# The words of the second MLP's weights loaded two steps in front instead of one, and four more of its weight tiles resident at its start

## The chip, the cores and the metric

The kernel runs on one core of one Trainium2 chip. The metric is the device time of one execution in microseconds (us), given as the median of several executions. The engines are named as the profile names them: PE (TensorE, the matmul engine), PEld (its weight loads), DVE (VectorE), ACT (ScalarE), POOL (GpSimd) and SP (SyncE); the last two issue most of the DMAs here.

## The reference, cut to what matters

Three parts follow one another: attention with a band mask (heads 0 to 3) and a dilated band mask (heads 4 to 7), an MLP that takes the maximum of three products, and an MLP with a rational activation.

```python
scores = (q @ k.T) / 8                      # 4 batches, 8 heads, 576 tokens, head size 64
scores = where(mask, scores, -1e9)          # 0 <= rel < 32; or 0 <= rel < 128 and rel % 4 == 0
attn = exp(scores - max); attn = attn / (attn.sum() + 1e-9)
x = (attn @ v)                              # arranged as 2304 tokens x 512

h = maximum(maximum(x @ w1, x @ w2), x @ w3)    # 512 -> 768
x = h @ w_out                                   # 768 -> 512

h = x @ w_in                                    # 512 -> 2048
P = a0 + a1*h + a2*h**2 + a3*h**3
Q = 1 + |b0|*|h| + |b1|*h**2
out = (P / (Q + 1e-6)) @ w_out2                 # 2048 -> 512
```

The weights come as 64-bit floating-point numbers. The kernel reads their raw words and makes 32-bit values of them itself.

## The kernel before, in words

Attention is cut into 12 chunks of 192 tokens (three a batch), the first MLP into units of 384, 384, 512, 512 and 512 tokens, the second MLP into 5 tiles of tokens by 16 slices of its inner size. Every value that enters an MLP's matmul is split into a high and a low part, and each product takes three matmuls (high by high, high by low, low by high: `mm3`, L581 to L586). An inner group of the first MLP is 12 matmuls, and its output group 18; a unit has 18 and 4 of them, which the code calls 22 slots. The order of each engine's instructions is the order in which the code emits them, moved by a scheduler that follows priorities; a block in `tc.high_priority(offset=-300)` has a lower one and is fitted in where its engine would be free.

Up to about 96 us a hand-written script mixes the first chunks of attention, unit 0, and the conversion of the first MLP's weights. Then units 1 to 4 follow. In units 1 to 3 the generator `attn(u + 1)` is advanced by one piece after each slot, so that the next unit's attention is computed between the groups: scores (L335), their masking, maximum and difference on DVE (L354 to L377), exponentials on ACT (L385), sums and scaling on DVE (L396 to L403), transposes on PE into the PSUM bank `tpp` (L414), their copy out of it on ACT to `pt` (L425), and the products with V (L437, L445), whose high part ACT writes to `x1h` (L462). For the MLP itself ACT copies one of three products to `m` (L604), DVE takes the maxima (L606), ACT and DVE split the result (`hhl`, L612 and L616), and ACT copies the unit's output to `xs` (L639).

Into the same units goes the conversion of the second MLP's 32 weight tiles of 128 by 512. A tile's steps are: `cv_load` issues a DMA of 512 KB on SP's queue that brings the raw words to a tile `raw`, of which there are two (L524); it is told to wait for the last matmul emitted so far (`PACE`); `cv_up` lets ACT turn the high words into `cvt` (L537); `cv_bits` does two operations on DVE (L543, L545), and `cv_lo` issues a DMA on POOL's queue that writes `cvt`, 256 KB, to scratch memory, `w2d` (L565). `cv_tick` (L573) advances all of these at once, each for another tile: 36 ticks over the 66 slots of units 1 to 3 (L770 to L773), in each of which tile k is loaded, tile k-1 goes through `cv_up`, k-2 through `cv_bits` and k-3 is written.

When unit 4 begins (L747 to L760), the space of conversion and attention is given back. The weight tiles come back from scratch by `load_w2` (L645): a DMA on SP's queue (L651), the high part by ACT (L652) and the low part by DVE (L653). Three are loaded there, and three more whenever one of the first MLP's six weight blocks is done with, 21 in all. The other 11 need the space of the pool `com`, which also holds `x1h` and `x1l`, the input of two units in turn; they are loaded when unit 4 has ended (L791 to L796), just ahead of the second MLP's first groups. Its work on a slice is one PE group into `h`, ACT and DVE operations (L819 to L856) that end in the high part `gh` (ACT, L851) and the low part `gl`, and the output matmuls (L870 to L872), which begin as soon as the first `gh` is there.

Of the kernel before, what the change touches and what calls it, by code (L numbers as in the profile page):

```python
# [7 lines left out]
F32 = mybir.dt.float32  # L8
F32R = mybir.dt.float32r
AF = mybir.ActivationFunctionType  # L10
# [93 lines left out]
def kernel(  # L104
# [16 lines left out]
    nc = tc.nc  # L121
# [35 lines left out]
    SBB = 1  # L157
    MB = 4
    LATE_CV = 300
    TICK = 36  # L160
    RAW2 = 2
    CVT2 = 2
    W2A = 3
# [5 lines left out]
    const = ctx.enter_context(tc.tile_pool(name="const", bufs=1))  # L169
    mm_p = ctx.enter_context(tc.tile_pool(name="mm", bufs=3, space=PSUM))  # L170

    com_es = ExitStack()
    com = com_es.enter_context(tc.tile_pool(name="com", bufs=1, reuse_waits="tile"))
    wo1_es = ExitStack()
# [45 lines left out]

    def unit_x1(u):
        if u not in x1:
            x1[u] = [com.tile([128, NP * T1], F32R, tag=tag, bufs=2, name=f"{tag}{u}")
                     [:, 0:NP * SZ1[u]].rearrange("p (c t) -> p c t", c=NP)
                     for tag in ("x1h", "x1l")]
        return x1[u]

    def load_k(b, part=None):

        if b not in at_k:  # L230
            if b == 0:
                for tag in ("x1h", "x1l"):
                    keys0[tag] = com.tile([128, NP * T1], F32, tag=tag, bufs=2, name="keys0")
                kTp, kTd = [keys0[tag][:, 0:2 * S] for tag in ("x1h", "x1l")]
            else:
                kTp, kTd = [at.tile([128, 2 * S], F32, tag=tag, name=f"{tag}{b}")
                            for tag in ("kTp", "kTd")]
            at_k[b] = (kTp.rearrange("p (n a t) -> p n a t", a=2, t=32),
                       kTd.rearrange("p (n m) -> p n m", n=8))
        kTp, kTd = at_k[b]  # L240
        queue = nc.sync if b < 2 else nc.gpsimd
        for k, cut in ((0, slice(0, CH // 32)), (2, slice(CH // 32, S // 32))):
            if part in (None, k):
                queue.dma_start(out=kTp[:, cut].rearrange("p n a t -> p (n a t)"),
                                in_=kp_in[b][:, 64 * cut.start:64 * cut.stop])
        if part in (None, 1):
            queue.dma_start(out=kTd.rearrange("p n m -> p (n m)"), in_=kd_in[b])
# [285 lines left out]
    def cv_up(i):  # L533
        t = cv_p[0].tile([128, 512], F32, tag="cvt", bufs=CVT2 if conv_seq[i][0] == "w2" else CVT,
                         name="cvt")
        cv[i][2] = t
        nc.scalar.activation(out=t, in_=cv[i][1].bitcast(F32), func=AF.Prelu, scale=SHRINK,  # L537
                             alpha=-(2.0 ** 32))

    def cv_bits(i):  # L540
        low, _, t, _ = cv[i]
        t = t.bitcast(I32)
        nc.vector.tensor_scalar(out=t, in0=t, scalar1=3, scalar2=None,  # L543
                                op0=ALU.logical_shift_left)
        nc.vector.scalar_tensor_tensor(out=t, in0=low, scalar=29, in1=t,  # L545
                                       op0=ALU.logical_shift_right, op1=ALU.bitwise_or)
# [23 lines left out]
    cv_steps = (("hi", cv_hi, "bits"), ("lo", cv_lo, "bits"), ("up", cv_up, "load"),  # L570
                ("bits", cv_bits, "up"), ("load", cv_load, None))

    def cv_tick(upto):  # L573

        was = dict(cv_at)
        for name, step, after in cv_steps:
            if was[name] < (upto if after is None else was[after]):
                step(was[name])
                cv_at[name] += 1

    def mm3(o, terms):  # L581
        n = len(terms)
# [59 lines left out]

    n2 = [0]

    def load_w2(pool):  # L645
        i = n2[0]
        n2[0] += 1
        _, side, c = order2[i]
        t = pool.tile([128, 1024], F32R, tag=f"w2_{i}", name=f"w2s{i}")
        raw = t[:, 512:1024].bitcast(F32)  # L650
        nc.sync.dma_start(out=raw, in_=w2d[i])  # L651
        nc.scalar.activation(out=t[:, 0:512], in_=raw, func=AF.Copy)  # L652
        nc.vector.tensor_sub(t[:, 512:1024], raw, t[:, 0:512].bitcast(F32))  # L653
        w2s[side, c] = t
# [17 lines left out]
    with ExitStack():  # L672
# [67 lines left out]
        for g in "pd":  # L740
            load_q(4, g)

        tick = 0
        for u in range(1, NU):
            last = u == NU - 1
            pieces = attn(u + 1) if not last else iter(())
            if last:  # L747
                while cv:
                    cv_tick(len(conv_seq))
                cv_es[0].close()  # L750
                at_es.close()
                x2_p = ctx.enter_context(
                    tc.tile_pool(name="x2", bufs=1, side="right", reuse_waits="tile"))
                w2a = ctx.enter_context(
                    tc.tile_pool(name="w2a", bufs=1, side="right", reuse_waits="tile"))
                with tc.high_priority(offset=-LATE_X2):
                    load_x2(0)
                with tc.high_priority(offset=-LATE_W2):
                    for _ in range(W2A):
                        load_w2(w2a)  # L760
            slot = 0
            groups = moe1(u)
            while True:
# [3 lines left out]
                kind, f, j = group  # L767
                slot += 1
                if not last:
                    tick += 1  # L770
                    if tick * TICK // 66 > (tick - 1) * TICK // 66:
                        with tc.high_priority(offset=-LATE_CV):
                            cv_tick(len(conv_seq))  # L773
                next(pieces, None)
                if last:
                    if slot in (8, 10, 12, 14):
# [260 lines left out]
```

## Time and profile before

| | |
|---|---|
| time, median of 3 runs (lowest, highest) | 793.21 us (792.85, 793.29) |
| the profiled execution's own time | 792.2 us |
| its span, first to last instruction | 790.4 us |
| PE busy | 775.4 us (98%), 4696 matmuls |
| DVE busy | 589.6 us (75%) |
| ACT busy | 461.0 us (58%) |
| POOL busy | 56.2 us (7%) |
| mean granted PE clock | 0.997 of full speed |
| DMA | 85.69 MB, mean 108 GB/s |

PE is busy for all but 15.0 us of the span. Between the span and the execution's own time lie 1.8 us; the median of the runs is 1.0 us above that execution. In all tables of the profile a wait is put down to what came last before the instruction could start.

### The profile page before, as it was taken

To read this page: it belongs to the slowest core of one execution; us is meant where nothing else is said; L and a number is where in the kernel's file an instruction comes from. 1 tells how busy PE (TensorE), PEld (TensorE's weight loads), DVE (VectorE), ACT (ScalarE), POOL (GpSimd) and SP (SyncE) were. 2 spreads that over 40 slices of the span, in tenths; PEclk is the share of its full clock that TensorE was granted. 3 is DMA by queue.
4 is the path that set the end of the run, shared out by engine and by line. 5 is a ranking of instruction groups with operands and counts; after the bars stand their busy time and mean duration, and the time that the engine had idled before them with its cause. 6 is when DMAs were issued, how large, how long until landed. Compare 5 with 4: busy or idle time off the path is not lost.

```text
span 790.4 us, 12266 instructions
## 1 busy us (share of the span) xinstructions
PE 775.4 (98%) x4696; PEld 671.2 (85%) x4696; DVE 589.6 (75%) x1053; ACT 461.0 (58%) x889; POOL 56.2 (7%) x107
## 2 busy tenths in 40 slices
PE   8999998999999999999989999999999999999997
PEld 7999997988788888888868888888888889989996
DVE  6999367466754664554199999888988889889885
ACT  5997234332332333433398768667776678777774
POOL 0000222121212110000100001000010001000000
PEclk9999999999999999999999999999999999999999
DMA  9963476576656451623600011000110011000001
GB/s 334 403 245 136 150 242 205 191 219 211 212 172 214 153 174 65 221 89 106 206 0 1 1 53 54 1 1 1 41 53 1 1 41 53 1 1 18 23 1 41
DMA packets 28267, 85.69 MB, mean 108 GB/s; under 512 B 3600, under 2 KB 5648, under 8 KB 28208
## 3 DMA queue, kind: packets, MB, share of 16 engines
q1 hardware_dynamic: 19488, 52.65, 19.6%
q0 software_dynamic: 8720, 32.25, 11.5%
q8 instruction: 37, 0.61, 0.3%
q14 instruction: 22, 0.18, 0.1%
HBM read 67.06 MB, written 17.83 MB: 107 GB/s over the span
## 4 chain that ended last, share of the span: by engine, by line
PE 91%; DMA 3%; DVE 3%; ACT 1%; issue 1%; SPq 0%; DVEq 0%; ACTq 0%
PE mm L584 12%; PE mm L585 12%; PE mm L586 11%; PE acc L872 8%; PE acc L871 8%; PE acc L870 8%; PE h L586 8%; PE h L584 8%; PE h L585 8%; PE sc L335 3%; DMA raw<-in_w_in_dram 2%; PE tpp L414 2%; PE pv L445 2%; PE pv L437 1%; DMA keys<-in_kd_dram 1%
## 5 line engine op out<-in xcount | busy, mean ns | idle before, releaser
L584 PE MATMUL mm<-x1h,w1s 128*128 128x512 f32 (+1 forms) x360 | 136.0, 378 | 0.0
L585 PE MATMUL mm<-x1l,w1s 128*128 128x512 f32 (+1 forms) x360 | 133.3, 370 | 0.0
L586 PE MATMUL mm<-x1h,w1s 128*128 128x512 f32 (+1 forms) x360 | 133.0, 369 | 0.0
L586 PE MATMUL h<-x2h,w2s 128*128 128x512 f32 (+1 forms) x320 | 117.7, 368 | 0.0
L584 PE MATMUL h<-x2h,w2s 128*128 128x512 f32 (+1 forms) x320 | 117.6, 368 | 0.0
L585 PE MATMUL h<-x2l,w2s 128*128 128x512 f32 (+1 forms) x320 | 117.6, 367 | 0.0
L870 PE MATMUL acc<-w2s,gh 128*128 128x512 f32 x288 | 112.2, 389 | 2.6 <-ACT gh L851 2.6
L871 PE MATMUL acc<-w2s,gh 128*128 128x512 f32 x288 | 112.3, 390 | 0.0
L872 PE MATMUL acc<-w2s,gl 128*128 128x512 f32 x288 | 109.3, 390 | 0.0
L826 DVE SCALAR_TENSOR_TENSOR q<-q,cs,ab 128x512 f32<-128x512 f32 (+1 forms) x80 | 55.8, 697 | 41.4 <-ACT ab L820 41.3
L819 ACT ACTIVATE q<-h 128x512 f32<-128x512 f32 (+1 forms) x80 | 43.9, 548 | 59.0 <-PE h L586 57.8
L584 PEld LDWEIGHTS mm<-x1h,w1s 128*128 128x128 f32 x360 | 68.0, 189 | 8.8
L586 PEld LDWEIGHTS mm<-x1h,w1s 128*128 128x128 f32 x360 | 68.0, 189 | 8.5
L585 PEld LDWEIGHTS mm<-x1l,w1s 128*128 128x128 f32 x360 | 68.1, 189 | 7.9
L585 PEld LDWEIGHTS h<-x2l,w2s 128*128 128x128 f32 x320 | 60.0, 188 | 8.2
L584 PEld LDWEIGHTS h<-x2h,w2s 128*128 128x128 f32 x320 | 60.1, 188 | 8.1
L586 PEld LDWEIGHTS h<-x2h,w2s 128*128 128x128 f32 x320 | 60.1, 188 | 7.5
L870 PEld LDWEIGHTS acc<-w2s,gh 128*128 128x128 f32 x288 | 54.1, 188 | 13.9 <-ACT gh L851 3.1
L851 ACT ACTIVATE gh<-p 128x512 fp32r<-128x512 f32 (+1 forms) x80 | 47.5, 593 | 31.1 <-DVE p L845 30.3
L872 PEld LDWEIGHTS acc<-w2s,gl 128*128 128x128 f32 x288 | 54.0, 188 | 11.2
L871 PEld LDWEIGHTS acc<-w2s,gh 128*128 128x128 f32 x288 | 54.1, 188 | 11.0
L821 ACT ACTIVATE p<-h,cs 128x512 f32<-128x512 f32 (+1 forms) x80 | 59.0, 737 | 0.0
(106 smaller groups left out, 1373.9 us busy)
## 6 DMA issues: line engine op xcount, KB each, us to landing
w1r<-in_w_dram SPq DMA_DIRECT2D x18, 512.0 KB, 9.2
raw<-in_w_in_dram SPq DMA_DIRECT2D x16, 512.0 KB, 4.5
w2d<-cvt POOLq DMA_DIRECT2D x32, 256.0 KB, 3.8
raw<-in_w_out_dram SPq DMA_DIRECT2D x16, 512.0 KB, 4.0
w2s<-w2d SPq DMA_DIRECT2D x32, 256.0 KB, 2.9
vd<-in_vd_dram POOLq DMA_DIRECT2D x8, 512.0 KB, 5.2
out_dram<-ob POOLq DMA_DIRECT2D x15, 256.0 KB, 2.7
wo1r<-in_w_out_dram SPq DMA_DIRECT2D x6, 512.0 KB, 8.3
```

What stands on the lines that cost most here:

```text
L335: nc.tensor.matmul(o[h], lhsT=l, rhs=r, start=not pem, stop=not pem or n % G == G - 1)
L414: nc.tensor.transpose(tp[:, i, :], sv[:, G * j + i, :], ident[:Q, :Q])
L584: nc.tensor.matmul(o, lhsT=lh, rhs=rh, start=(i == 0), stop=False)
L585: nc.tensor.matmul(o, lhsT=lh, rhs=rl, start=False, stop=False)
L586: pe_at[0] = nc.tensor.matmul(o, lhsT=ll, rhs=rh, start=False, stop=(i == n - 1))
L819: nc.scalar.activation(out=s["q"], in_=s["h"], func=AF.Square)
L821: nc.scalar.activation(out=s["p"], in_=s["h"], func=AF.Identity, scale=cs[:, 3:4], bias=cs[:, 2:3])
L826: nc.vector.scalar_tensor_tensor(out=s["q"], in0=s["q"], scalar=cs[:, 5:6], in1=s["ab"], op0=ALU.mult, op1=ALU.add)
L851: nc.scalar.activation(out=s["gh"], in_=s["p"], func=AF.Copy)
L870: nc.tensor.matmul(o, lhsT=gh, rhs=w[:, 0:512], start=(c == 0), stop=False)
L871: nc.tensor.matmul(o, lhsT=gh, rhs=w[:, 512:1024], start=False, stop=False)
L872: nc.tensor.matmul(o, lhsT=gl, rhs=w[:, 0:512], start=False, stop=(c == F2 - 1))
```

## The change

The conversion is no longer a pipeline of ticks. A step, `w2_words(k)`, does everything for tile k, up, bits and write, and then issues the load of tile k+2; the first two loads are issued ahead of unit 1. `WORDS` says how many steps lie in each unit (9, 11 and 12, spread over 22 slots). `cv_up` gets the same kind of dependency as the load: it waits for the last matmul that is emitted at its place.

The two pairs of buffers for `x1h` and `x1l` are parted: units 1 and 3 (and the keys of the first batch) use a new pool `xa`, units 0, 2 and 4 the pool `com`. When unit 4 begins, `xa` is free, and four weight tiles, `w2x`, two in each of its buffers, are loaded into it. So 25 tiles are there or on their way during unit 4, and 7 wait for the space of `com`.

```diff
--- before.py
+++ after.py
@@ -157,7 +157,7 @@
     SBB = 1
     MB = 4
     LATE_CV = 300
-    TICK = 36
+    WORDS = {1: 9, 2: 11, 3: 12}
     RAW2 = 2
     CVT2 = 2
     W2A = 3
@@ -169,6 +169,7 @@
     const = ctx.enter_context(tc.tile_pool(name="const", bufs=1))
     mm_p = ctx.enter_context(tc.tile_pool(name="mm", bufs=3, space=PSUM))
 
+    xa = ctx.enter_context(tc.tile_pool(name="xa", bufs=1, reuse_waits="tile"))
     com_es = ExitStack()
     com = com_es.enter_context(tc.tile_pool(name="com", bufs=1, reuse_waits="tile"))
     wo1_es = ExitStack()
@@ -220,7 +221,7 @@
 
     def unit_x1(u):
         if u not in x1:
-            x1[u] = [com.tile([128, NP * T1], F32R, tag=tag, bufs=2, name=f"{tag}{u}")
+            x1[u] = [(xa if u % 2 else com).tile([128, NP * T1], F32R, tag=tag, name=f"{tag}{u}")
                      [:, 0:NP * SZ1[u]].rearrange("p (c t) -> p c t", c=NP)
                      for tag in ("x1h", "x1l")]
         return x1[u]
@@ -230,7 +231,7 @@
         if b not in at_k:
             if b == 0:
                 for tag in ("x1h", "x1l"):
-                    keys0[tag] = com.tile([128, NP * T1], F32, tag=tag, bufs=2, name="keys0")
+                    keys0[tag] = xa.tile([128, NP * T1], F32, tag=tag, name="keys0")
                 kTp, kTd = [keys0[tag][:, 0:2 * S] for tag in ("x1h", "x1l")]
             else:
                 kTp, kTd = [at.tile([128, 2 * S], F32, tag=tag, name=f"{tag}{b}")
@@ -534,8 +535,10 @@
         t = cv_p[0].tile([128, 512], F32, tag="cvt", bufs=CVT2 if conv_seq[i][0] == "w2" else CVT,
                          name="cvt")
         cv[i][2] = t
-        nc.scalar.activation(out=t, in_=cv[i][1].bitcast(F32), func=AF.Prelu, scale=SHRINK,
-                             alpha=-(2.0 ** 32))
+        up = nc.scalar.activation(out=t, in_=cv[i][1].bitcast(F32), func=AF.Prelu, scale=SHRINK,
+                                  alpha=-(2.0 ** 32))
+        if conv_seq[i][0] == "w2":
+            tc.add_manual_dep(up.ins, pe_at[0].ins.name, PACE, reason="not ahead of its words")
 
     def cv_bits(i):
         low, _, t, _ = cv[i]
@@ -570,13 +573,14 @@
     cv_steps = (("hi", cv_hi, "bits"), ("lo", cv_lo, "bits"), ("up", cv_up, "load"),
                 ("bits", cv_bits, "up"), ("load", cv_load, None))
 
-    def cv_tick(upto):
-
-        was = dict(cv_at)
-        for name, step, after in cv_steps:
-            if was[name] < (upto if after is None else was[after]):
-                step(was[name])
-                cv_at[name] += 1
+    def w2_words(k):
+
+        i = n_w1 + k
+        cv_up(i)
+        cv_bits(i)
+        cv_lo(i)
+        if k + RAW2 < 2 * F2:
+            cv_load(i + RAW2)
 
     def mm3(o, terms):
         n = len(terms)
@@ -642,11 +646,12 @@
 
     n2 = [0]
 
-    def load_w2(pool):
+    def load_w2(pool, t=None):
         i = n2[0]
         n2[0] += 1
         _, side, c = order2[i]
-        t = pool.tile([128, 1024], F32R, tag=f"w2_{i}", name=f"w2s{i}")
+        if t is None:
+            t = pool.tile([128, 1024], F32R, tag=f"w2_{i}", name=f"w2s{i}")
         raw = t[:, 512:1024].bitcast(F32)
         nc.sync.dma_start(out=raw, in_=w2d[i])
         nc.scalar.activation(out=t[:, 0:512], in_=raw, func=AF.Copy)
@@ -740,13 +745,14 @@
         for g in "pd":
             load_q(4, g)
 
-        tick = 0
+        for k in range(RAW2):
+            cv_load(n_w1 + k)
+        words = 0
         for u in range(1, NU):
             last = u == NU - 1
             pieces = attn(u + 1) if not last else iter(())
             if last:
-                while cv:
-                    cv_tick(len(conv_seq))
+                assert not cv
                 cv_es[0].close()
                 at_es.close()
                 x2_p = ctx.enter_context(
@@ -758,6 +764,10 @@
                 with tc.high_priority(offset=-LATE_W2):
                     for _ in range(W2A):
                         load_w2(w2a)
+                    for tag in ("x1h", "x1l"):
+                        t = xa.tile([128, NP * T1], F32R, tag=tag, name="w2x")
+                        load_w2(xa, t[:, 0:1024])
+                        load_w2(xa, t[:, 1024:2048])
             slot = 0
             groups = moe1(u)
             while True:
@@ -767,10 +777,10 @@
                 kind, f, j = group
                 slot += 1
                 if not last:
-                    tick += 1
-                    if tick * TICK // 66 > (tick - 1) * TICK // 66:
+                    if slot * WORDS[u] // 22 > (slot - 1) * WORDS[u] // 22:
                         with tc.high_priority(offset=-LATE_CV):
-                            cv_tick(len(conv_seq))
+                            w2_words(words)
+                        words += 1
                 next(pieces, None)
                 if last:
                     if slot in (8, 10, 12, 14):
```

In the excerpts of the order below, lines are those of each kernel's own file (L538 after is L537 before, L426 is L425, L608 L604, L616 L612, L643 L639, L657 and L658 are L652 and L653). A name in brackets is the engine or the DMA queue (DMAHW: of SP, DMASW: of POOL) whose event the row waits for.

ACT in unit 1, second of its three chunks, before:

```order
L612 ACTIVATE hhl_1665<-m 128x384 [waits DVE_49]
L537 ACTIVATE cvt<-raw 128x512 [waits DMAHW5_49,DMASW1_49]
L604 ACTIVATE m<-mm 128x384 [waits DMASW3_49,PE_49,Activation_49]
L425 ACTIVATE pt<-tpp 96x384 [waits PE_49,Activation_49]
L537 ACTIVATE cvt<-raw 128x512 [waits DMAHW6_49,DMASW7_49]
L385 ACTIVATE sb<-sb 96x640 [waits DVE_49]
L425 ACTIVATE pt<-tpp 96x384 [waits PE_49]
L612 ACTIVATE hhl_1775<-m 128x384 [waits DVE_49]
L537 ACTIVATE cvt<-raw 128x512 [waits DMAHW7_49,DMASW0_49]
L604 ACTIVATE m<-mm 128x384 [waits PE_49]
L425 ACTIVATE pt<-tpp 80x384 [waits PE_49,Activation_49]
```

and the same stretch after:

```order
L616 ACTIVATE hhl_1674<-m 128x384 [waits DVE_49]
L608 ACTIVATE m<-mm 128x384 [waits DMASW3_49,PE_49,Activation_49]
L538 ACTIVATE cvt<-raw 128x512 [waits DMAHW5_49,DMASW1_49]
L426 ACTIVATE pt<-tpp 96x384 [waits PE_49,Activation_49]
L426 ACTIVATE pt<-tpp 96x384 [waits PE_49]
L386 ACTIVATE sb<-sb 96x640 [waits DVE_49]
L616 ACTIVATE hhl_1777<-m 128x384 [waits DVE_49]
L608 ACTIVATE m<-mm 128x384 [waits PE_49]
L426 ACTIVATE pt<-tpp 80x384 [waits PE_49,Activation_49]
L538 ACTIVATE cvt<-raw 128x512 [waits DMAHW6_49,DMASW7_49]
L426 ACTIVATE pt<-tpp 80x384 [waits PE_49]
```

Of the three conversions before, the first stands between the split `hhl` and the copy to `m`, the third between the next two of these. After there are two, each behind the copy to `m`, and the last `pt` has one right ahead of it.

ACT at the end of unit 3, before:

```order
L385 ACTIVATE sb<-sb 96x640 [waits DVE_49]
L604 ACTIVATE m<-mm 128x512 [waits PE_49,Activation_49]
L425 ACTIVATE pt<-tpp 96x384 [waits PE_49]
L612 ACTIVATE hhl_3491<-m 128x512 [waits DVE_49]
L639 ACTIVATE xs<-mm 128x512 [waits PE_49,Activation_49]
L425 ACTIVATE pt<-tpp 80x384 [waits PE_49,Activation_49]
L425 ACTIVATE pt<-tpp 80x384 [waits PE_49]
L639 ACTIVATE xs<-mm 128x512 [waits PE_49,Activation_49]
L462 ACTIVATE x1h_2987<-pv 128x2x192 [waits PE_49] x2
L639 ACTIVATE xs<-mm 128x512 [waits PE_49,Activation_49]
```

and after:

```order
L616 ACTIVATE hhl_3481<-m 128x512 [waits DVE_49]
L657 ACTIVATE w2x<-w2x 128x512 [waits DMAHW1_49,PE_49]
L643 ACTIVATE xs<-mm 128x512 [waits PE_49,Activation_49]
L426 ACTIVATE pt<-tpp 80x384 [waits PE_49,Activation_49]
L538 ACTIVATE cvt<-raw 128x512 [waits DMAHW7_49,DMASW3_49]
L657 ACTIVATE w2x<-w2x 128x512 [waits DMAHW2_49]
L426 ACTIVATE pt<-tpp 80x384 [waits PE_49]
L657 ACTIVATE w2x<-w2x 128x512 [waits DMAHW3_49]
L657 ACTIVATE w2x<-w2x 128x512 [waits DMAHW4_49]
L643 ACTIVATE xs<-mm 128x512 [waits PE_49,Activation_49]
L463 ACTIVATE x1h_2975<-pv 128x2x192 [waits PE_49] x2
L643 ACTIVATE xs<-mm 128x512 [waits PE_49,Activation_49]
```

The four `w2x` and one more conversion now stand among the copies of `xs` and `pt`; the first `w2x` waits for its DMA and stands ahead of `xs`.

DVE at the second MLP's start, before:

```order
L828 TENSOR_TENSOR p<-h,p 128x512 [waits Activation_49]
L653 TENSOR_TENSOR w2s_4158<-w2s_4158 128x512 [waits DMAHW5_49,Activation_49]
L653 TENSOR_TENSOR w2s_4162<-w2s_4162 128x512 [waits DMAHW6_49,Activation_49]
L653 TENSOR_TENSOR w2s_4166<-w2s_4166 128x512 [waits DMAHW7_49,Activation_49]
L829 SCALAR_TENSOR_TENSOR p<-p,mk,h 128x512 [waits DVE_49]
L653 TENSOR_TENSOR w2s_4170<-w2s_4170 128x512 [waits DMAHW0_49,Activation_49]
L653 TENSOR_TENSOR w2s_4174<-w2s_4174 128x512 [waits DMAHW1_49,Activation_49]
L653 TENSOR_TENSOR w2s_4178<-w2s_4178 128x512 [waits DMAHW2_49,Activation_49]
L653 TENSOR_TENSOR w2s_4182<-w2s_4182 128x512 [waits DMASW7_49,DMAHW3_49,DMASW4_49,Activation_49]
L841 SCALAR_TENSOR_TENSOR q<-q,r 128x512
```

and after:

```order
L838 TENSOR_TENSOR p<-h,p 128x512 [waits Activation_49]
L658 TENSOR_TENSOR w2s_4175<-w2s_4175 128x512 [waits DMAHW1_49,Activation_49]
L658 TENSOR_TENSOR w2s_4179<-w2s_4179 128x512 [waits DMAHW2_49,Activation_49]
L658 TENSOR_TENSOR w2s_4183<-w2s_4183 128x512 [waits DMASW7_49,DMAHW3_49,DMASW4_49,Activation_49]
L839 SCALAR_TENSOR_TENSOR p<-p,mk,h 128x512 [waits DVE_49]
L851 SCALAR_TENSOR_TENSOR q<-q,r 128x512 [waits Activation_49]
```

Seven splits stand between the product at the top and `q<-q,r` before, three after.

## Rows read from the trace of the kernel before

**Rows 1.** Stretches (columns: stretch, us, each engine's busy us (xinstructions), PEclk, DMA share, GB/s)

```profile
96.00:252.00 156.00, 150.57 (x1204) 131.85 (x1202) 96.46 (x191) 54.80 (x107) 33.28 (x61) 0.99 0.63 209
252.00:400.00 148.00, 148.00 (x803) 122.69 (x803) 73.18 (x122) 54.66 (x98) 10.83 (x20) 1.00 0.42 140
400.00:412.00 12.00, 9.36 (x42) 7.39 (x41) 12.00 (x21) 11.45 (x21) 0.00 (x0) 1.00 0.00 0
412.00:785.00 373.00, 373.00 (x1733) 319.82 (x1732) 333.14 (x554) 274.69 (x486) 8.01 (x15) 1.00 0.05 18
```

**Rows 2.** Waits of TensorE: engine, line, releaser: us in total, times, longest

```profile
PE acc L870 <- ACT gh L851: 2.6, 1, 2.6
PE tpp L414 <- ACT pt L425: 2.6, 2, 1.3
PE tpp L414 <- ACT cvt L537: 2.2, 1, 2.2
```

**Rows 3.** Instruction groups (line engine op tiles xcount | busy, mean ns | idle before, releaser)

```profile
L543 DVE TENSOR_SCALAR cvt<-cvt 128x512 int32<-128x512 int32 x56 | 23.5, 420 | 47.2 <-ACT cvt L537 46.8
...
L545 DVE SCALAR_TENSOR_TENSOR cvt<-raw,cvt 128x512 int32<-128x512 int32 x32 | 22.0, 688 | 0.7
...
L537 ACT ACTIVATE cvt<-raw 128x512 f32<-128x512 f32 x32 | 21.3, 666 | 59.8 <-DMA raw<-in_w_in_dram 37.2 <-DMA raw<-in_w_out_dram 22.5
```

**Rows 4.** Tile raw: issues from one matrix (first and last start), landing of all

```profile
L524 SPq DMA_DIRECT2D raw<-in_w_in_dram x16: 328/328/331, 92.6 to 271.8; - x16
...
DMA to landing us min/median/max: 3.5/4.1/7.6
```

**Rows 5.** Line 565: landing of the converted tiles in scratch

```profile
DMA to landing us min/median/max: 2.3/3.8/6.9
```

**Rows 6.** Line 651: landing of the weight tiles from scratch

```profile
DMA to landing us min/median/max: 2.5/2.9/5.7
```

**Rows 7.** Timeline, unit 1, second chunk (start us, us, engine line op tiles [idle before <-releaser])

```profile
111.16 0.33 SPq L524 DMA_DIRECT2D raw<-in_w_in_dram  x1
...
118.85 0.66 ACT L537 ACTIVATE cvt<-raw 128x512 f32<-128x512 f32 x1 [3.96 <-DMA raw<-in_w_in_dram]
...
120.31 0.53 PE L414 MATMUL tpp<-mk,sb 128*96 128x128 f32 x3 [1.29 <-ACT pt L425]
...
126.57 0.65 ACT L537 ACTIVATE cvt<-raw 128x512 f32<-128x512 f32 x1
...
127.22 0.51 PE L414 MATMUL tpp<-mk,sb 96*80 96x96 f32 x4 [2.20 <-ACT cvt L537]
```

**Rows 8.** Timeline, unit 2, a plain chunk's end

```profile
206.71 0.66 ACT L537 ACTIVATE cvt<-raw 128x512 f32<-128x512 f32 x1 [4.09 <-DMA raw<-in_w_in_dram]
...
208.80 0.53 PE L414 MATMUL tpp<-mk,sb 96*80 96x96 f32 x4 [1.33 <-ACT pt L425]
```

**Rows 9.** Stretches of 1 us behind the longest gap

```profile
127.00:128.00 1.00, 0.78 (x6) 0.81 (x7) 0.97 (x4) 0.77 (x3) 0.00 (x0) 0.79 0.96 369
128.00:129.00 1.00, 1.00 (x5) 0.87 (x4) 0.61 (x1) 0.31 (x1) 0.10 (x1) 0.50 1.01 410
```

**Rows 10.** Timeline, start of the second MLP

```profile
401.84 2.49 DVE L653 TENSOR_TENSOR w2s<-w2s 128x512 fp32r<-128x512 f32 x4
...
405.15 0.39 PE L586 MATMUL h<-x2h,w2s 128*128 128x512 f32 x1
...
407.49 0.63 ACT L851 ACTIVATE gh<-p 128x512 fp32r<-128x512 f32 x1
...
408.17 0.50 PE L870 MATMUL acc<-w2s,gh 128*128 128x512 f32 x1 [2.64 <-ACT gh L851]
```

**Rows 11.** Timeline, end of unit 3

```profile
304.46 0.39 PE L586 MATMUL mm<-x1h,w1s 128*128 128x512 f32 x1
...
309.03 0.60 ACT L639 ACTIVATE xs<-mm 128x512 f32<-128x512 f32 x1 [2.79 <-PE mm L586]
...
310.06 0.52 PE L414 MATMUL tpp<-mk,sb 96*80 96x96 f32 x4
```

## The prediction

> **What bounds the kernel now.** I read the stretches first, since a sum over the whole span hides where PE stands. From 252 to 400 us and from 412 to 785 us PE is busy for the whole stretch (148.00 of 148.00 us, 373.00 of 373.00) [rows 1]: nothing that ACT, DVE or a queue does there can save time, only cost it. Two stretches have room: from 96 to 252 us PE is busy for 150.57 of 156.00, so 5.43 us are idle, and from 400 to 412 us for 9.36 of 12.00, 2.64 us idle [rows 1].
>
> Next the list of PE's waits. In the first of these stretches it names the copies `pt` (2.6 us, twice) and one conversion (2.2 us), all ahead of transposes [rows 2]; the remaining 0.6 us of the 5.43 are short. In the second it is one wait of 2.6 us for `gh` [rows 2]. The groups then say what ACT itself had waited for: L537 has 59.8 us of idle time ahead of it, every bit put down to the DMA that brings the raw words [rows 3]. ACT is an engine with little to do in these units (54.80 of 156 us [rows 1]), but it works in order, and whoever stands behind a waiting L537 waits along.
>
> The timeline shows how that reaches PE. The words' load is issued at 111.16, ACT reaches the conversion and is idle for 3.96 us until it starts at 118.85; the `pt` behind it comes late, and PE waits 1.29 us at 120.31. At 126.57 the same happens once more and PE waits 2.20 us at 127.22 [rows 7]. In unit 2 ACT waits 4.09 us for the words at 206.71, and PE 1.33 us at 208.80 [rows 8]. So the load, issued one step ahead, is late against ACT's order, and only where transposes follow closely does PE feel it.
>
> **Term 1: loads two steps ahead.** Of 16 loads from one matrix the first is issued at 92.6 us and the last at 271.8 [rows 4]. They run from the first load to the 28th of all 32 (the sequence takes three tiles of the first matrix and then alternates), so a step is 179.2 / 27 = 6.6 us, and two steps 13 us on the average. A load lands after 3.5 to 7.6 us, 4.1 in the median [rows 4]. The closest pair of steps in the new plan (22 slots for 12 words, unit 3) is three slots; a slot has 12 matmuls of about 0.215 us (373.00 us for 1733 [rows 1]), so 7.7 us without the attention's own pieces. In unit 1 (9 words) a pair is at least four slots of three quarters that length, also 7.7 us. Even the slowest landing fits, though only just, and the median has 3.6 us to spare. I take the raw words' wait as gone, with all of the 5.43 us of idle time: -5.4. The bounds are 0 (the waits stay) and -5.43.
>
> What is late next? The new order puts a tile's conversion on ACT, both bit operations on DVE and the write on POOL's queue right behind each other: 0.666 + 0.420 + 0.688 us [rows 3]. These instructions are the same 32 times three as before; only their places change. I replayed the two chunks with the waits by hand from the rows' durations: the dilated group's `pt` then has 0.5 to 1.1 us in hand over PE, an estimate. The write of a tile lands after at most 6.9 us [rows 5], and its `cvt` buffer is wanted two steps later, at 7.7 us or more: no wait. The dependency added to `cv_up` holds ACT until PE has finished a group; queued behind it are copies of that same group's or later banks, which would wait for PE as well: nothing, if my replay is right (what it costs if not is the slower rival).
>
> **Term 2: the clock behind the longest gap.** After the 2.20 us of waiting the granted clock falls: 0.79 in the stretch from 127 to 128 us, 0.50 in the next, which is the lower level of 1.2 GHz, and 0.50 in two more like it; then it is back at 1.00 [rows 9]. In PE's work this loses 0.21 + 3 x 0.50 = 1.7 us; the last stretch may be part of the return, so I count 1.6. The gaps of 1.29 and 1.33 us were followed by no such fall. With the 2.20 us gap gone the loss goes: -1.6 (bounds 0 and -1.7).
>
> **Term 3: four splits fewer at the second MLP's start.** At 401.84 us DVE does four splits in a row, 2.49 us, ahead of the chain to the first `gh` (407.49), on which PE waits until 408.17 [rows 10]. The order shows the four gone from just this place, three staying. ACT's four splits go too, so neither engine holds the other back. DVE's share comes to 2.41 us (the next operation starts 0.08 us before the splits' modelled end), and `gh` starts at 405.08. The last h group's final matmul starts at 405.15 and takes 0.39 [rows 10], so 405.54 is the earliest that PE could be free; it would wait 408.17 - 2.41 - 405.54 = 0.22 us instead of 2.64. That is -2.4, with bounds of 0 and -2.64.
>
> **Term 4: the four splits come back at the end of unit 3.** The buffers of `xa` are free when unit 3's last inner matmul has run, 304.46 + 0.39 = 304.85 us [rows 11]. The loads queue on SP behind that wait. One split stands on ACT ahead of the `xs` that starts at 309.03, in front of which ACT was idle for 2.79 us [rows 11]. With the median landing of 2.9 us [rows 6] it is ready at 307.8 and done by 308.4: it fits into the idle time. With the slowest, 5.7, it is done at 311.2, and `xs` and the `pt` behind it come 2.2 us late; the transposes that need that `pt` start at 310.06 [rows 11], with next to nothing in hand. Cost 0 to 2.2; I take +0.3, near the median landing, since four loads are issued one behind the other, where others in the trace are issued three at a time. Beside the row stands the Trainium skill, "DMA: Bandwidth & Descriptors", section "Anatomy of one DMA": a transfer takes about 2.0 us and its bytes at 436 GB/s, which for 256 KB is 2.6 us (an estimate from that page, whose fit is for transfers issued by POOL); by it the term would be 0. The rows' 2.9 decides. The loads of `x2l` and the first three tiles go behind the `w2x` on SP's queue, some 4 us before they matter to a matmul; in unit 4 PE is busy throughout [rows 1]: 0.
>
> **The sum.** 792.2 - 5.4 - 1.6 - 2.4 + 0.3 = 783.1 us, made against the profiled execution. The median of the runs lies 1.0 us above it, so the time forecast is 784.1 us.
>
> **Rivals.** *Partial:* the mechanism is right, but new gaps of the old size come up. Two transposes still wait 1.3 us each, and half of term 3 stays because ACT becomes what `gh` waits for: 784.1 + 2.6 + 1.2 = 787.9. For it: the replay's margins of 0.5 to 1.1 us are thin, and the first wait that is taken away often shows the next. Against it: ACT is busy for a third of the stretch [rows 1].
>
> *The lead does not help:* the loads are late not because they are issued late but because the DMAs are full. In the stretch from 128 to 129 us their share is 1.01 at 410 GB/s [rows 9]; were each load's landing to stretch to two steps, 13 us against a maximum of 7.6 now, terms 1 and 2 would vanish and the `w2x` come late too: 784.1 + 5.4 + 1.6 + 1.9 = 793.0, no change. Against it: the mean share from 96 to 252 us is 0.63 [rows 1], and the rate of loads stays one a step. The Trainium skill has a rule on this side, "DMA: Bandwidth & Descriptors", section "Issuing engines are not separate DMA queues": DMAs of SP and POOL run on the same 16 engines and interleave. The full stretch agrees; by the rule a deeper lead brings no more bandwidth, only time to wait in.
>
> *Slower:* the new dependency holds ACT at each of the 32 steps until PE ends a group, and the `pt` behind it, once the conversion's 0.67 us have passed, reaches PE late. The price is 32 times what the wait exceeds the slack by. Terms 1 to 3 give back 9.1 us net, so it decides at 9.1 / 32 = 0.28 us a step; at 0.4 us it is 784.1 + 12.8 = 796.9. For it: the last `pt` in the new order of the second chunk has a conversion right ahead of it. Against it: slack is uneven, and most steps are not next to a transpose.
>
> **How the numbers follow.** Forecast as worked out 0.62, partial 0.20, no help 0.09, slower 0.09. A difference under 0.2% (1.6 us) is about what a measurement of this kernel cannot tell from no change. So faster is 0.82, the same 0.09, slower 0.09. The likeliest case's own range is 782.3 (all terms at their ends, 792.2 + 1.0 - 5.43 - 1.7 - 2.64 = 783.4, and 1.1 for the runs' scatter and what a replay by hand leaves out) to 787. The range up to 790.0 takes in the partial case and holds eight in ten.
>
> **What would show it.** In the profile after: PE's idle time from 96 to 252 us below 1 us; no idle time for raw words ahead of the conversion, or less than 5 us of it in total; no stretch with a granted clock of 0.50 in unit 1; PE's wait for the first `gh` below 0.5 us; a possible gap of a few tenths near 310 us. The prediction is wrong if `tpp` still waits for `pt` by more than 2 us in total, if ACT's idle time ahead of the conversion is now put down to PE and returns in the transposes' waits, or if `x2l` and the weight tiles make PE wait in unit 4.

## The result, and the profile after

The changed kernel takes 783.49 us (median of 5 runs, 783.28 to 785.21) where the kernel before took 792.85 beside it (median of 5, 791.86 to 793.29); the ratio is 0.9889 with an interval from 0.9874 to 0.9903. The forecast was 784.1 us. The profiled execution took 783.45 us with a span of 781.6.

The stretches of the changed kernel, with the same columns as [rows 1], answer to the first three of those:

```profile
96.00:252.00 156.00, 156.00 (x1244) 137.44 (x1243) 98.39 (x192) 55.64 (x107) 32.22 (x59) 1.00 0.65 201
252.00:400.00 148.00, 146.56 (x795) 121.02 (x794) 82.47 (x137) 62.91 (x113) 12.09 (x22) 1.00 0.46 146
400.00:412.00 12.00, 12.00 (x55) 9.88 (x54) 12.00 (x20) 11.25 (x19) 0.00 (x0) 1.00 0.01 1
```

From 96 to 252 us PE now has no idle time at all. A new 1.44 us of it stands between 252 and 400 us. What PE waits for there is in its list of waits (engine, line, releaser: total, times, longest), in answer to [rows 2]:

```profile
PE tpp L415 <- ACT pt L426: 1.2, 1, 1.2
...
PE acc L880 <- ACT gh L861: 0.2, 1, 0.2
```

So the wait for the first `gh` has gone from 2.6 to 0.2 us, and one wait of transposes for `pt` is left. The groups of the conversion, in answer to [rows 3], show what became of ACT's own wait:

```profile
L546 DVE TENSOR_SCALAR cvt<-cvt 128x512 int32<-128x512 int32 x56 | 23.8, 424 | 27.6 <-ACT cvt L538 27.1
...
L538 ACT ACTIVATE cvt<-raw 128x512 f32<-128x512 f32 x32 | 21.3, 666 | 32.4 <-PE mm L590 32.3
```

No idle time ahead of L538 is put down to the words any more; 32.3 us are put down to PE, that is to the dependency that holds the conversion to its place (the hold, from here on). The words themselves land no sooner, after 3.9 to 7.1 us, 4.2 in the median (3.5, 7.6 and 4.1 in [rows 4]).

The profiled executions differ by 792.2 - 783.45 = 8.75 us. PE's idle time accounts for -5.43 (96 to 252 us), -2.40 (first `gh`: 2.64 to 0.24) and +1.21 (end of unit 3), together -6.6. PE's busy time falls from 775.4 to 773.2, by 2.2: the half clock of [rows 9] is gone (the clock is 1.00 in each 10 us from 96 to 256), 1.6 to 1.7 us of it; the other half microsecond I leave open.

The new wait, in the timeline of the changed kernel (start us, us, engine line op tiles [idle before <-releaser]):

```profile
297.16 2.25 SPq L656 DMA_DIRECT2D w2x<-w2d  x4
...
302.02 0.63 ACT L657 ACTIVATE w2x<-w2x 128x512 fp32r<-128x512 f32 x1 [3.64 <-DMA w2x<-w2d]
...
302.56 0.58 ACT L643 ACTIVATE xs<-mm 128x512 f32<-128x512 f32 x1
...
303.03 0.47 ACT L426 ACTIVATE pt<-tpp 80x384 f32<-80x384 f32 x1
...
303.56 0.53 PE L415 MATMUL tpp<-mk,sb 96*80 96x96 f32 x4 [1.21 <-ACT pt L426]
```

The four loads go out from 297.16 on, right behind one of raw words (296.74) and a write of a converted tile on POOL's queue (296.97). The first split starts 4.9 us later, `xs` and `pt` queue behind it on ACT, and the transposes wait 1.21 us. The place is the one that [rows 11] showed; only the landing, after 4.8 to 5.3 us, is later than the 2.9 us counted.

### The profile page after: what moved, and what is told of

Its sections match the earlier page's. It is cut to its first block, busy times and chain, and to the rows that moved or that the text cites. A ratio compares the mean times of both kernels' runs of the same rounds, so it can differ in the third digit from the quotient of the medians.

```text
span 781.6 us, 12256 instructions
## 1 busy us (share of the span) xinstructions
PE 773.2 (99%) x4696; PEld 670.3 (86%) x4696; DVE 591.9 (76%) x1053; ACT 462.7 (59%) x889; POOL 56.5 (7%) x107
## 3 DMA queue, kind: packets, MB, share of 16 engines
q0 software_dynamic: 8720, 32.25, 11.3%
## 4 chain that ended last, share of the span: by engine, by line
PE 94%; ACT 2%; DMA 1%; DVE 1%; issue 0%; SPq 0%; ACTq 0%
PE mm L588 13%; PE mm L589 12%; PE mm L590 12%; PE acc L881 8%; PE acc L880 8%; PE acc L882 8%; PE h L588 8%; PE h L589 8%; PE h L590 8%; PE sc L336 3%; PE tpp L415 2%; PE pv L446 2%; PE pv L438 1%; DMA keys<-in_kd_dram 1%; DMA w2x<-w2d 1%
## 5 line engine op out<-in xcount | busy, mean ns | idle before, releaser
L590 PE MATMUL h<-x2h,w2s 128*128 128x512 f32 (+1 forms) x280 | 102.9, 368 | 0.0
L588 PE MATMUL h<-x2h,w2s 128*128 128x512 f32 (+1 forms) x280 | 102.9, 368 | 0.0
L589 PE MATMUL h<-x2l,w2s 128*128 128x512 f32 (+1 forms) x280 | 102.9, 367 | 0.0
L881 PE MATMUL acc<-w2s,gh 128*128 128x512 f32 x252 | 98.3, 390 | 0.0
L880 PE MATMUL acc<-w2s,gh 128*128 128x512 f32 x252 | 98.0, 389 | 0.0
L882 PE MATMUL acc<-w2s,gl 128*128 128x512 f32 x252 | 96.0, 390 | 0.0
L588 PEld LDWEIGHTS mm<-x1h,w1s 128*128 128x128 f32 x360 | 67.6, 188 | 8.8
L590 PEld LDWEIGHTS mm<-x1h,w1s 128*128 128x128 f32 x360 | 67.6, 188 | 8.6
L610 DVE TENSOR_TENSOR m<-mm,m 128x512 f32<-128x512 f32 (+1 forms) x60 | 38.0, 634 | 34.4 <-PE mm L590 29.0
L588 PEld LDWEIGHTS h<-x2h,w2s 128*128 128x128 f32 x280 | 52.5, 188 | 7.1
L589 PEld LDWEIGHTS h<-x2l,w2s 128*128 128x128 f32 x280 | 52.6, 188 | 7.0
L590 PEld LDWEIGHTS h<-x2h,w2s 128*128 128x128 f32 x280 | 52.5, 188 | 6.6
L855 DVE SCALAR_TENSOR_TENSOR p<-p,mk,r 128x512 f32<-128x512 f32 (+1 forms) x80 | 55.7, 696 | 1.6
L845 ACT ACTIVATE r<-q,cs 128x512 f32<-128x512 f32 (+1 forms) x80 | 55.0, 687 | 3.0 <-DVE q L836 1.0
```

The lines of the kernel that those rows point to most:

```text
L588: nc.tensor.matmul(o, lhsT=lh, rhs=rh, start=(i == 0), stop=False)
L589: nc.tensor.matmul(o, lhsT=lh, rhs=rl, start=False, stop=False)
L590: pe_at[0] = nc.tensor.matmul(o, lhsT=ll, rhs=rh, start=False, stop=(i == n - 1))
L845: nc.scalar.activation(out=s["r"], in_=s["q"], func=AF.Ln, scale=LS, bias=cs[:, 6:7])
L855: nc.vector.scalar_tensor_tensor(out=s["p"], in0=s["p"], scalar=co[:, 0:1], in1=s["r"], op0=ALU.subtract, op1=ALU.mult)
L880: nc.tensor.matmul(o, lhsT=gh, rhs=w[:, 0:512], start=(c == 0), stop=False)
```

## The experiments

**Each part alone.** `e1` has the new conversion and none of the early tiles; `e2` has the tiles and the old ticks; `a0` is the changed kernel again. All ran on one chip with the kernel before, which took 793.3 us there (790.3 to 797.48).

```diff
 e1, against the changed kernel:
-            x1[u] = [(xa if u % 2 else com).tile([128, NP * T1], F32R, tag=tag, name=f"{tag}{u}")
+            x1[u] = [com.tile([128, NP * T1], F32R, tag=tag, bufs=2, name=f"{tag}{u}")
...
-                    for tag in ("x1h", "x1l"):
-                        t = xa.tile([128, NP * T1], F32R, tag=tag, name="w2x")
-                        load_w2(xa, t[:, 0:1024])
-                        load_w2(xa, t[:, 1024:2048])
 e2, against the kernel before: these lines the other way round, cv_tick and TICK kept
```

> The new conversion alone; the input buffers of the units are in one pool as before, and no weight tile is loaded early, so 11 tiles wait for the second MLP's start. By the theory that the parts add up: no idle time of PE from 96 to 252 us and no half clock (both as after), the wait for the first gh back at about 2.6 us, no gap at the end of unit 3: 783.5 + 2.4 - 1.2 = 784.7 us. By the rival that the early tiles carry most of the gain: 790 or more, with PE idle in unit 1.

> The four early tiles alone, with the conversion in ticks as before. If the parts add up: PE still idle for about 5.4 us from 96 to 252 us, the half clock behind the 2.2 us gap still there, the wait for the first gh at about 0.2 instead of 2.6 us, and 0 to 1.2 us of a new gap at the end of unit 3: 792.85 - 2.4 + (0 to 1.2) = 790.5 to 791.7 us. By the rival that the wait for gh only hides another (ACT, the next h group): 792 to 793.

> The changed kernel again, on the same chip as these three, for the comparison among them: 783.5 us (783.3 to 785.2).

`e1` took 786.23 us (784.23 to 787.0; ratio 0.9906, 0.9877 to 0.9935), `e2` 790.43 (788.49 to 792.86; 0.9960, 0.9942 to 0.9979), `a0` 783.26 (782.69 to 783.74; 0.9874, 0.9847 to 0.9901). From 793.3 the conversion gives -7.1, the tiles -2.9, both together -10.0: the parts add up, to within the scatter of the runs. In `e1` PE is busy for 156.00 of 156.00 us from 96 to 252 and waits 2.6 us for `gh`; in `e2` it is idle for 4.77 us (151.23 busy), and waits 0.2 for `gh`. At the end of unit 3 the same four loads cost `e2` less than the changed kernel, 0.33 us:

```profile
303.69 1.75 SPq L653 DMA_DIRECT2D w2x<-w2d  x4
...
306.46 1.27 ACT L654 ACTIVATE w2x<-w2x 128x512 fp32r<-128x512 f32 x2 [1.18 <-DMA w2x<-w2d]
...
309.82 0.53 PE L415 MATMUL tpp<-mk,sb 96*80 96x96 f32 x4 [0.33 <-ACT pt L426]
```

Here no other load or write has been issued for 4.1 us when they go out (the last was a write, at 299.59), and they land after 2.7 to 3.9 us. `e1` came out 1.5 us above what was expected, for a reason that the stretches around its `gh` wait show (same columns as above):

```profile
398.00:400.00 2.00, 0.79 (x4) 0.33 (x2) 2.00 (x5) 1.57 (x3) 0.00 (x0) 1.00 0.00 0
400.00:402.00 2.00, 0.57 (x2) 0.47 (x3) 2.00 (x5) 1.97 (x4) 0.00 (x0) 0.91 0.00 0
402.00:404.00 2.00, 2.00 (x7) 1.54 (x5) 2.00 (x4) 1.97 (x4) 0.00 (x0) 0.50 0.00 0
404.00:406.00 2.00, 2.00 (x8) 1.64 (x7) 2.00 (x4) 1.92 (x4) 0.00 (x0) 0.74 0.00 0
```

The granted clock falls to 0.50 behind this 2.6 us gap, as it had done behind the gap in unit 1 of the kernel before [rows 9], where it did not fall behind the wait for `gh`. It differs from execution to execution: of `e1`'s six, the two with a mean clock of 0.999 took 784.23 and 784.30 us, as expected, and the four with 0.997 took 786.22 to 787.0. The slowest is the profiled one, in which PE also waited 2.0 us for the first keys at the start (0.8 in the changed kernel's).

**Lead or hold.** The change does two things to a conversion: its load goes out a step earlier, and a dependency holds it behind its slot's group. Three kernels part them. `e3` keeps the hold and goes back to one step of lead; `e4` keeps the two steps and drops the hold; `h1` is the kernel before with the hold and nothing else.

```diff
 e3, against the changed kernel (one load ahead of unit 1):
+        if k + 1 < 2 * F2:
+            cv_load(i + 1)
         cv_up(i)
         cv_bits(i)
         cv_lo(i)
-        if k + RAW2 < 2 * F2:
-            cv_load(i + RAW2)
 e4, against the changed kernel (h1 adds the same lines to the kernel before):
-        if conv_seq[i][0] == "w2":
-            tc.add_manual_dep(up.ins, pe_at[0].ins.name, PACE, reason="not ahead of its words")
```

> The changed kernel with the load of word k+1, not k+2, issued in step k (at the same place as before, behind the same group); conversions held and adjoining as in the change. If the lead is what took PE's waits away, ACT's idle time for raw words comes back (10 to 40 us in total, since a step of 6.6 us on the average and as little as one slot in unit 3 stands against landings of 3.9 to 7.1) and with it 1 to 5 us of PE: 785 to 788 us. By the rival that holding and joining the conversions did it: no such idle time, 783.3 us.

> The changed kernel without the dependency that holds cv_up to its group; loads two steps ahead as in the change. If the lead alone does it: no PE idle time from 96 to 252 us, 783.3 us (to 784.5). By the rival that the hold is needed, since without it the conversions stand further forward in ACT's order, ahead of the words' landing: idle time of ACT for raw words of 10 us or more, PE idle again for 2 to 5 us, 785.5 to 789 us.

> The kernel before with one dependency more: cv_up is held behind the last matmul emitted at its place; ticks, one step of lead, buffers and tiles as before. By the theory that the hold is what took PE's waits away, and the second step of lead adds little: ACT's idle time for raw words falls from 59.7 us to under 10, PE's idle time from 96 to 252 us from 5.4 to about 1 us, and the time by 4 to 6 us to 787 to 789 us; the 2.6 us ahead of the first gh stay. By the rival that the joined steps or the lead are needed beside it: PE idle for 3 us or more there, 790.5 to 793 us.

| kernel | hold | lead | ACT idle for words, us | PE idle 96 to 252, us | time, us (ratio, interval) |
|---|---|---|---|---|---|
| before | no | 1, in ticks | 59.7 | 5.43 | 792.85 |
| `e4` | no | 2, joined | 67.6 | 3.12 | 788.17 (0.9930, 0.9906 to 0.9953) |
| `h1` | yes | 1, in ticks | 8.0 | 1.53 | 787.23 (0.9931, 0.9908 to 0.9954) |
| `e3` | yes | 1, joined | 1.7 | 1.15 | 785.28 (0.9900, 0.9874 to 0.9927) |
| changed | yes | 2, joined | 0 | 0.00 | 783.49 (0.9889, 0.9874 to 0.9903) |

(Joined: up, bits and write of a tile are emitted together, as in the change. `e3`, `e4` and the changed kernel have the early tiles, worth 2.9 us; the other two have not. The ratios are against the kernel before on the same chip.) The conversion's group in each, `e4`, `h1` and `e3`:

```profile
L538 ACT ACTIVATE cvt<-raw 128x512 f32<-128x512 f32 x32 | 21.3, 667 | 68.6 <-DMA raw<-in_w_out_dram 42.6 <-DMA raw<-in_w_in_dram 25.0 <-DMA w2d<-cvt 0.9
```

```profile
L537 ACT ACTIVATE cvt<-raw 128x512 f32<-128x512 f32 x32 | 21.3, 665 | 35.6 <-PE mm L588 27.4 <-DMA raw<-in_w_in_dram 6.2 <-DMA raw<-in_w_out_dram 1.8
```

```profile
L538 ACT ACTIVATE cvt<-raw 128x512 f32<-128x512 f32 x32 | 21.3, 666 | 34.4 <-PE mm L590 32.3 <-DMA raw<-in_w_in_dram 1.7 <-DVE x2l L675 0.2
```

What matters in these lines is who is named as the releaser. Without the hold ACT stands for the words longer than in the kernel before, although they are loaded two steps ahead; with it, and one step of lead, it hardly does. `e4`'s timeline in unit 1 shows how two steps come to nothing:

```profile
112.36 0.33 SPq L525 DMA_DIRECT2D raw<-in_w_out_dram  x1
```

```profile
112.46 0.69 ACT L386 ACTIVATE sb<-sb 128x576 f32<-128x576 f32 x1 [2.93 <-DVE sb L373]
118.67 0.68 ACT L538 ACTIVATE cvt<-raw 128x512 f32<-128x512 f32 x1 [5.52 <-DMA raw<-in_w_out_dram]
...
126.25 0.52 ACT L614 ACTIVATE hhl<-m 128x384 fp32r<-128x384 f32 x1 [1.65 <-DVE m L608]
```

```profile
119.38 0.43 DVE L544 TENSOR_SCALAR cvt<-cvt 128x512 int32<-128x512 int32 x1 [3.75 <-ACT cvt L538]
```

```profile
127.33 0.50 PE L415 MATMUL tpp<-mk,sb 96*80 96x96 f32 x4 [2.05 <-DVE sb L404]
```

The load goes out at 112.36; ACT, done with the exponentials at 113.15, has the conversion of these words as its next instruction, and stands for 5.52 us. In the changed kernel the load of the same words, the fifth, goes out at nearly the same time, and their conversion comes 11.3 us behind it:

```profile
113.42 0.33 SPq L525 DMA_DIRECT2D raw<-in_w_out_dram  x1
```

```profile
124.71 0.66 ACT L538 ACTIVATE cvt<-raw 128x512 f32<-128x512 f32 x1
```

So without the hold the scheduler had moved the conversion forward in ACT's order, while the load stayed tied to PE. Everything behind it shifts: DVE stands 3.75 us for the converted words, and PE waits 2.05 us at 127.33, put down to DVE, further down the chain. `e3` is the small remainder that the second step takes away: one wait of 1.7 us for words, and PE idle for 1.15 us behind it. Neither expectation for `e3` was met as a whole: the idle time for words is near that of the rival, PE's idle time and the time are in the range of the lead. The times alone do not tell `e3` from the changed kernel, for the intervals of their ratios overlap; three of `e3`'s executions took 783.6 to 784.6 us, among them the profiled one, and three 786.0 to 787.1, of which no trace is kept. The remainder rests on the profile.

**How much of the wait for `gh` goes with each tile.** `e7` parts only the buffers of `x1h`, so that two tiles come early.

```diff
-            x1[u] = [(xa if u % 2 else com).tile([128, NP * T1], F32R, tag=tag, name=f"{tag}{u}")
+            x1[u] = [(xa if u % 2 and tag == "x1h" else com).tile([128, NP * T1], F32R, tag=tag, bufs=1 if tag == "x1h" else 2, name=f"{tag}{u}")
...
-                    for tag in ("x1h", "x1l"):
-                        t = xa.tile([128, NP * T1], F32R, tag=tag, name="w2x")
-                        load_w2(xa, t[:, 0:1024])
-                        load_w2(xa, t[:, 1024:2048])
+                    t = xa.tile([128, NP * T1], F32R, tag="x1h", name="w2x")
+                    load_w2(xa, t[:, 0:1024])
+                    load_w2(xa, t[:, 1024:2048])
```

> The changed kernel with two early tiles in place of four (only x1h is parted; x1l stays in one pool), so that 9 tiles wait for the second MLP's start. If each split on DVE ahead of the first gh costs its 0.6 us: PE waits there for 0.2 + 2 x 0.6 = 1.4 us (against 0.2 with four tiles and 2.6 with none), and the 1.2 to 1.4 us near 303 us stay, since the first split still stands ahead of xs: 783.3 + 1.2 = 784.5 us. By the rival that the wait is set by something else once two splits are gone: 0.2 us there, 783.3 us. On the clock: no granted clock under 0.999 if a gap of 1.4 us is too short to make it fall; executions with 0.997 and 1.6 us more if gaps of that size can do it too.

It took 784.44 us (784.22 to 784.94; ratio 0.9887, 0.9867 to 0.9906), and its waits read

```profile
PE tpp L415 <- ACT pt L426: 1.6, 1, 1.6
PE acc L879 <- ACT gh L860: 1.4, 1, 1.4
```

With none, two and four early tiles the wait is 2.6, 1.4 and 0.2 us: 0.6 us a split, as the DVE rows gave. None of its four executions had a mean clock under 0.999; in the profiled one the two gaps are 1.4 and 1.6 us. The two early loads land after 5.1 to 5.3 us, as late as the four of the changed kernel.

**The splits held back.** In `f1` the loads stay, and the splits of `w2x` wait for a group in the middle of unit 4.

```diff
...
+    def split_w2(t, late=False):
+        raw = t[:, 512:1024].bitcast(F32)
+        hi = nc.scalar.activation(out=t[:, 0:512], in_=raw, func=AF.Copy)
+        if late:
+            tc.add_manual_dep(hi.ins, pe_at[0].ins.name, PACE, reason="not ahead of unit 3")
+        nc.vector.tensor_sub(t[:, 512:1024], raw, t[:, 0:512].bitcast(F32))
...
+                    if slot in (9, 11, 13, 15):
+                        with tc.high_priority(offset=-LATE_W2):
+                            split_w2(w2x.pop(0), True)
```

> The changed kernel, with the w2x loads where they were, but their splits on ACT and DVE held back into the middle of unit 4. If the 1.2 us gap near 302 us comes from the split that waits on ACT for its DMA ahead of xs and pt, it goes: 783.5 - 1.2 = 782.3 us. By the rival that pt is late for another reason (the xs that waits for PE): 783.5 us.

It took 781.83 us (781.24 to 782.28; ratio to the kernel before 0.9855, 0.9825 to 0.9884), 1.4 less than `a0` on the same chip, and no run of the one lies within the other's. PE has no idle time left from 96 to 390 us:

```profile
96.00:252.00 156.00, 156.00 (x1246) 137.54 (x1246) 98.76 (x192) 55.48 (x108) 32.10 (x59) 1.00 0.64 202
252.00:390.00 138.00, 138.00 (x759) 114.40 (x758) 73.32 (x122) 54.75 (x98) 12.03 (x22) 1.00 0.48 156
```

This is the fastest version, and its mean clock was 1.0 in each of six executions.

**Gaps made on purpose.** Two kernels, `g5` and `g8`, were to give PE one gap of about 1.3 and one of about 2.8 us. Each is `f1` with a copy of transposed scores repeated on ACT.

```diff
-                nc.scalar.activation(out=pt, in_=tp, func=AF.Copy)
+                for _ in range(6 if (c, g, j) == (5, "d", 0) else 1):    # 9 in the other
+                    nc.scalar.activation(out=pt, in_=tp, func=AF.Copy)
```

> The kernel with late splits, and in chunk 5 one copy of a transposed tile repeated five more times on ACT, so that PE waits once, for an estimated 1.0 to 1.6 us near 128 us. By the theory that a gap of PE as long as 2.2 us or more makes the clock fall and one of about 1.3 does not: 781.8 + 1.3 = 783.1 us, all granted clocks at 0.999 or 1.0. By the rival that the fall has nothing to do with the gap's length: some executions with 0.997, 1.6 us longer.

> The same with eight more copies: one gap of an estimated 2.5 to 3.1 us near 128 us. By the theory of the gap's length: the clock falls to 0.50 behind it for about 3 us in most executions, 781.8 + 2.8 + 1.6 = 786.2 us with a mean clock of 0.997 or 0.998. By the rival that the fall in the kernel before came from other work beside it (the full DMA engines, DVE): no fall, 784.6 us at a clock of 1.0.

They took 781.68 us (781.52 to 783.58) and 783.33 (782.12 to 784.01), and tell nothing of the clock: the gap did not come about. The order of PE's work gave way, the dilated group's products with V moved behind other matmuls (in `g8` they begin at 131.9 us), and PE's list of waits names no copy. Which gaps make the clock fall has to be read from the others.

## Why the prediction was right, point by point

**Term 1, the size: right.** It counted all 5.43 us of idle time from 96 to 252 us, and all of it went.

**Term 1, the cause: wrong.** The prediction put it down to loads two steps ahead, and of the new dependency it said that it costs nothing; that it could gain something was not considered. The table shows the reverse: the dependency alone (`h1`) takes PE's idle time from 5.43 to 1.53 us, while the second step of lead, with the steps joined, but without the dependency (`e4`) leaves 3.12 and makes ACT stand longer than before. The failed step is the reading of "one step in front" as a time. The prediction worked out 6.6 us a step from the loads' issue times, compared it with the landing, and took it that the conversion comes as many steps behind its load as the code says; but its place was the scheduler's, which had put it forward. With the conversion tied to its slot, one step nearly does. That all of the 5.43 us went is in this respect luck: the change holds the conversion as well, for a reason that the sum did not count. Had the hold been left out, the forecast of 784.1 would have been 4 us too low.

**Term 2, the clock: right in this pair.** The half clock in unit 1 is gone. But the kernel before had two gaps, of 2.2 and 2.6 us, and `e1` and `h1` show that the clock can fall behind the second as well. The executions of the kernel before on the second chip had mean clocks from 0.991 (797.48 us) to 0.999 (790.3 and 791.55), the changed kernel's there 0.999 to 1.0. So the single execution with one fall stood for a mean over executions with fewer and more; where the falls of those with 0.991 to 0.995 lay is not shown, for no trace of them is kept. 9.4 us were gained on the first chip, 10.0 on the second.

**Term 3, the first `gh`: right.** 0.22 us was worked out, 0.24 came; `e7` confirms the price of a split.

**Term 4: the right place, mis-sized.** It counted 0.3 us in a range of 0 to 2.2; 1.21 came, 1.4 in `a0`, and `f1` gives 1.4 back. The step that failed is "near the median landing", which takes the four loads by themselves. By themselves they do cost 0.33 us (`e2`). In the changed kernel the new plan puts a load of words (512 KB) and the write of a converted tile (256 KB) right ahead of them, and the first was used 4.9 us after its issue. The loads behind the first are not what made it late, for with two in place of four the landing is the same (`e7`). That it is these two transfers is argued from what differs between `e2` and the changed kernel; no run takes them away alone. From 300 to 302 us the DMA engines of the changed kernel were full (last two columns: share, GB/s):

```profile
300.00:302.00 2.00, 2.00 (x13) 1.61 (x11) 0.00 (x0) 0.00 (x0) 0.00 (x0) 1.00 1.02 399
```

The estimate of 2.6 us from the Trainium skill ("DMA: Bandwidth & Descriptors", section "Anatomy of one DMA") would have put the cost at 0. The quickest landing in `e2`, 2.7 us, comes near it; in the changed kernel, with the other transfers beside, none was under 4.8, and the measurement decides.

**The sum.** Against the profiled execution 783.1 us was forecast and 783.45 came: term 4 was 0.9 too small, and PE's busy time fell by 0.6 more than term 2 said. The 1.0 us added for the runs did not come up again, since their median lies at 783.49. That the forecast of 784.1 is only 0.6 us off is partly errors that cancel.

**The rivals.** None took place as a whole in the changed kernel. Of the partial one a single wait of the old size came up, 1.21 us, and not where it was looked for; of the second, only that the `w2x` land late, while the words land as before. The third was argued from the right instruction, for ACT does stand for 32.3 us on PE's groups; but PE is not idle once from 96 to 252 us, and so it cost nothing there. A likely reason is that what stands behind the conversion is mostly bound to the same groups; this is argued, not shown.

What stays open: half a microsecond of PE's busy time between the two profiled executions, and how the 1.53 us that `h1` leaves divide between the joining of the steps and the second step of lead (`e3`, with 1.15, differs from `h1` in the early tiles too, and ran on another chip).

## What to carry to other kernels

A prefetch distance counted in program steps is worth little unless the consumer is tied to its place (here the longer distance and the joined steps took 2.3 of 5.43 us without that, and the tie alone 3.9); where a scheduler orders the engines, look at where the consumer stands in its engine's order against the time at which the load is issued. Work moved out of one crowded place is late or early somewhere else: the four splits cost 1.2 us where they went first (0.3 where the order had no other transfer beside their loads), and nothing once they were held back to a stretch with room. When an idle gap of PE is taken away, count with it what the clock may lose behind it, from several executions rather than from one.

## What the runs showed of the hardware

The fall of the granted clock behind a gap of PE is not certain in an execution: behind the 2.6 us gap of `e1` it came in the profiled one (0.50 for about 3 us), and four of six executions had a mean clock of 0.997 and took 1.9 to 2.8 us more than the two with 0.999. The twelve profiled executions have seven gaps of 2.0 us or more. Behind four of them the clock fell to 0.50: 2.20 us in the kernel before, 2.21 in `e2`, 2.64 in `e1` and 2.63 in `h1`. Behind three it did not: 2.64 us in the kernel before, 2.05 in `e4`, and 2.03 at the start of `e1`. Behind the shorter ones there is no fall in any of the twelve. Of the executions of the three kernels whose profiled gaps are 1.2 to 1.6 us (the changed kernel, `a0`, `e7`) 14 of 15 had a mean clock of 0.999 or more; one of the changed kernel's had 0.997 (785.21 us), and without its trace it can't be said where.

PE's wait for the first keys, a DMA at the start, was 0.3 to 2.0 us in the twelve profiled executions, though none of the edits changes what is loaded there (0.8 and 0.3 in the two of the changed kernel). It is likely a part of the scatter between executions of one kernel, beside the clock.
